# Decay rows picked by matmuls with a single one, and the rounding of whole heads on VectorE, in a fused attention and two-MoE-layer kernel

## The chip, the cores and the metric

One core of one Trainium2 chip. The time is the device time of one execution in microseconds; the runs of a kernel are given by their median. [...]

## The reference

Attention with decay over 4 batches, 8 heads, 576 positions, head size 64, then two feed-forward layers over the 2304 rows of 512 values. All in fp32.

```python
scores = (q @ k.T) / 8
cum    = cumsum(log(clip(f, 1e-4, 1)))            # one row per batch and head
scores = where(causal, -1e9, scores + cum[i] - cum[j])
attn   = softmax(scores);  x = attn @ v           # heads side by side: 2304 x 512
x = (relu(x @ w_in1) ** 2) @ w_out1               # d_ff 2048
x = elu(x @ w_in2) @ w_out2
```

## The kernel before, in words

**Scores with the decay inside.** A head's operand has the 64 rows of q (or k), transposed, and four more rows, 64 to 67, that carry cum and ones, so that one matmul over 68 rows gives scores plus decay. The table `ca` (32 rows, one for each batch and head, with 4 x 512 values: two of 8 cum for q's first 256 columns, two of -8 cum for k's, high and low part of each, ones elsewhere) is made at the start by `split_c` on VectorE (L229 to L232). Positions 256 to 575 have their rows in a DRAM tensor `aug`.

**Two kinds of heads.** Batch 0 is "plain" (`PLAIN = (0,)`): its q and k go into the matmul as fp32, unrounded. Batches 1 to 3 are split: `load_head` with part "F" (a whole head) rounds the raw tile 128x1280 to fp32r into `qk1` (`copy(ENG["qk"][w], ...)`, L126), GpSimd subtracts to get the low parts of q and k (`minus`, L135), a transfer on SP's queue copies k's high part into `qk2`, and another one brings the decay rows. `ENG` says for each step which engine does it for the parts A, B, F: 'a' ScalarE, 'v' VectorE, 'p' GpSimd, 'd' a transfer; `w = "ABF".index(part)`.

**Order of the work.** Batch 0 is done in two passes (`SPLIT = (0,)`): first part A (the first 256 rows) of all eight heads, steps 0 to 7, then for each pair of heads the last 64 rows ("4") and part B. The other batches go through A, A, 4, B, B for each pair. In each step `soft` computes scores, minima and exponentials of one item, `outs` transposes, multiplies by v and folds the item of the step before (`LAG = 1`). Heads are fetched `FETCH = 4` and loaded `AHEAD = 2` steps ahead. Between them `fill()` runs pieces of the first feed-forward layer (`unit`: 256 rows against half of the weights) as a credit by `PACE` and `COST` allows; unit 0 needs all heads of part A. Until it has started, `fill()` issues two or three matmuls on zeros (`busy`, L250), and before everything there are `WARM = 60` of them. From the instructions traced this way a scheduler with a timing model makes each engine's order; an engine runs its instructions in that order.

**Weights.** A half of the first layer's weights comes in as 64-bit words; `words` makes 32-bit ones from it in a tile `wt` (pool `xa`, tag "o", two buffers, shared by other short-lived tiles of that pool): an absolute value on ScalarE (L153), four steps on VectorE (L154 to L157), then rounding on ScalarE (L173) and a subtraction on GpSimd (L135). `W_AT` sets how many halves each step starts.

**The rows of part A.** In `fetch_plain`, for the first head of each pair, SP's queue fetches q and k of both heads (L275) and v (L278) into one tile, and ScalarE's queue issues two transfers (L277) that bring each head's four decay rows from `ca` into partitions 64 to 67 of that tile. `ca` lies one head to a partition, and the four rows must come to four partitions. The scores of part A (`soft_a`, L346) read them.

**Copies.** `copy(eng, dst, x)` is one instruction: ScalarE activation Copy (L126), GpSimd (L128), VectorE tensor_copy (L130). `ps_t` is the PSUM pool with three buffers of tag "t" in which transposes are written.

The lines around the change:

```python
ENG = {'qk': 'aaa', 'ql': 'ppp', 'kh': 'pvd', 'kl': 'ppp', 'vh': 'ppp', 'vl': 'ppp', 'xl': 'pv'}
nc.sync.dma_start(out=t[0:64, 0:1024], in_=first[h // 2])                                         # L275
for i in range(2):
    nc.scalar.dma_start(out=t[64:68, 512 * i:512 * i + 512], in_=f32(ca[g + i:g + i + 1]))       # L277
copy(ENG["qk"][w], qk1, raw[:, ac])                                                              # load_head, part F
```

Of the kernel before, what the change touches and what calls it, by code (L numbers as in the profile page):

```python
# [10 lines left out]
F32 = mybir.dt.float32  # L11
F32R = mybir.dt.float32r
I32 = mybir.dt.int32
AF = mybir.ActivationFunctionType
ALU = mybir.AluOpType

B, H, S, D = 4, 8, 576, 64
# [25 lines left out]
PLAIN = (0,)  # L43

PLAIN_B = 4
CP = {'pA': 'a', 'pB': 'av', 'xA': 'a', 'xB': 'a'}
ENG = {'qk': 'aaa', 'ql': 'ppp', 'kh': 'pvd', 'kl': 'ppp', 'vh': 'ppp', 'vl': 'ppp', 'xl': 'pv'}
NORM = 'ap'
GL = 'pv'
SQ = 'appp'  # L50
# [22 lines left out]
def f32(ap):  # L73
    return ap.bitcast(F32)
# [10 lines left out]
def attention_then_moe_kernel(ctx, tc, first, firstv, plain, qkv, aug0, f, w1, w2, out):  # L85
    nc = tc.nc
    PS = bass.MemoryType.PSUM

    def pool(stack, name, bufs, side, **kw):
        return stack.enter_context(tc.tile_pool(name=name, bufs=bufs, side=side, reuse_waits="tile", **kw))  # L90
# [5 lines left out]
    xa = pool(ctx, "xa", 2, "left")  # L96
# [21 lines left out]
    def minus(eng, dst, x, hi):  # L118
        if eng == "p":
            less(dst, x, hi)  # L120
        else:
            nc.vector.tensor_tensor(dst, x, f32(hi), op=ALU.subtract)

    def copy(eng, dst, x, scale=None):
        if eng == "a":
            nc.scalar.activation(out=dst, in_=x, func=AF.Copy, scale=1.0 if scale is None else scale)  # L126
        elif eng == "p":
            nc.gpsimd.tensor_scalar(dst, x, 1.0 if scale is None else scale, 0.0, op0=ALU.mult, op1=ALU.add)  # L128
        elif scale is None:
            nc.vector.tensor_copy(dst, x)  # L130
        else:
            nc.vector.tensor_scalar(dst, x, scale, None, op0=ALU.mult)
# [65 lines left out]
    ps_t = pool(at, "ps_t", PSB[1], "right", space=PS)  # L198
# [14 lines left out]
    e4s = [a1.tile([128, 640], F32, name=f"e4_{s}") for s in range(2)]  # L213
    me = getattr(nc, MEM)
    ca = wa.tile([B * H, 4, 512], F32R, tag="w7", name="ca")
    me.memset(f32(ca), 1.0)
    nc.gpsimd.memset(mz, 0.0)
    mask(mz[:, 384:512], [[-1, 128]])
# [37 lines left out]
    pairs = {}  # L256

    def fetch_head(b, h, part):
        if b in PLAIN and (part == "A" or h // 2 < PLAIN_B):
            fetch_plain(b, h, part)  # L260
            return
        raw = ab.tile([128, ALL], F32, tag="raw", name="raw", bufs=BUFS["raw"])
        raws[b, h, part] = raw
        nc.sync.dma_start(out=raw, in_=qkv[b, h])

    def fetch_plain(b, h, part):
        g = b * H + h
        k = h % 2
        if part == "A":
            if k == 0:  # L270
                if h // 2 < BUFS["raw"]:
                    t = ab.tile([128, ALL], F32, tag="raw", name="rawA", bufs=BUFS["raw"])
                else:
                    t = hd.tile([128, RAW], F32, tag="qk1", name="rawA", bufs=BUFS["qs"])
                nc.sync.dma_start(out=t[0:64, 0:1024], in_=first[h // 2])  # L275
                for i in range(2):
                    nc.scalar.dma_start(out=t[64:68, 512 * i:512 * i + 512], in_=f32(ca[g + i:g + i + 1]))  # L277
                nc.sync.dma_start(out=t[:, 1024:1280], in_=firstv[h // 2])  # L278
                pairs[b, h // 2] = t
            t = pairs[b, h // 2]  # L280
            raws[b, h, part] = Plain(t, 512 * k - Q0, 512 * k + 256, t[:, 1024 + 128 * k:1152 + 128 * k].rearrange("p (j d) -> p j d", d=D))
            return
        if k == 0:
            t = ab.tile([128, ALL], F32, tag="raw", name="rawB", bufs=BUFS["raw"])
        else:
            t = hd.tile([128, RAW], F32, tag="qk1", name="rawC", bufs=BUFS["qs"])
        nc.sync.dma_start(out=t[0:64, 0:RAW], in_=plain[h])
        nc.sync.dma_start(out=t[64:68, 0:RAW], in_=aug[g])
        if k == 0:
            v = t[:, RAW:ALL]  # L290
        else:
            v = hd.tile([128, 5 * D], F32, tag="vv", name="vp", bufs=BUFS["vv"])
        nc.sync.dma_start(out=v, in_=qkv[b, h, :, RAW:ALL])
        raws[b, h, part] = Plain(t, 0, QW, v.rearrange("p (j d) -> p j d", d=D))

    def aug_split():
        cp, cn = (ab.tile([32, 2, S - 256], F32R, tag="eb", name=t, bufs=BUFS["eb"]) for t in ("cp", "cn"))
        split_c(cp, cn, slice(256, S))
        return cp, cn
# [6 lines left out]
    def load_head(b, h, part):  # L306
# [12 lines left out]
        if part == "A":  # L319
            ac = slice(Q0, QW + 256)  # L320
            copy(ENG["qk"][w], qk1[:, ac], raw[:, ac])
        else:
            ac = slice(0, RAW)
            if part == "F":
                copy(ENG["qk"][w], qk1, raw[:, ac])
            else:
                copy(ENG["qk"][w], qk1[:, qc], raw[:, qc])
                copy(ENG["qk"][w], qk1[:, kc], raw[:, kc])
        if part == "A":
            nc.sync.dma_start(out=f32(qk2[64:68, ac]), in_=f32(ca[g:g + 1]))  # L330
        else:
            nc.sync.dma_start(out=f32(qk2[64:68, ac]), in_=aug[g, :, ac])
        minus(ENG["ql"][w], qk2[0:64, qc], raw[0:64, qc], qk1[0:64, qc])
        if ENG["kh"][w] == "d":
            nc.sync.dma_start(out=f32(qk2[0:64, kc]), in_=f32(qk1[0:64, kc]))
# [8 lines left out]
    def scores(dst, hh, q0, j0, n, first, last):  # L344
        if isinstance(hh, Plain):
            seen[0] = nc.tensor.matmul(out=dst, lhsT=hh.t[0:68, hh.q + q0:hh.q + q0 + 128],  # L346
                                       rhs=hh.t[0:68, hh.k + j0:hh.k + j0 + n], start=first, stop=last)
            return
        qk1, qk2 = hh[0:2]
        nc.tensor.matmul(out=dst, lhsT=qk1[:, q0:q0 + 128], rhs=qk1[:, QW + j0:QW + j0 + n], start=first, stop=False)  # L350
        seen[0] = nc.tensor.matmul(out=dst, lhsT=qk2[0:68, q0:q0 + 128], rhs=qk2[0:68, QW + j0:QW + j0 + n], start=False, stop=last)  # L351

    def reduce_min(e, s, m, nm, init=BIG):
        nc.vector.tensor_tensor_reduce(out=e, in0=s, in1=m, scale=-0.125, scalar=init, op0=ALU.add, op1=ALU.min, accum_out=nm)

    def expo(e, nm, z):
        nc.scalar.activation(out=e, in_=e, func=AF.Exp, bias=nm, scale=-1.0, accum_out=z)
# [7 lines left out]
    def sums(kind, b, hp, k):  # L365
        if k == 0:
            zs[kind, b, hp] = ab.tile([128, 2, 2], F32, tag="z" + kind, name="z" + kind, bufs=3)
        return zs[kind, b, hp][:, :, k]

    def soft_a(b, h, hh):  # L370
        e = ab.tile([128, 384], F32, tag="ea", name="ea", bufs=BUFS["ea"])
        nm = ab.tile([128, 2], F32, tag="nm2", name="nm2", bufs=3)
        z = sums("A", b, h // 2, h % 2)
        s = ps_s.tile([128, 512], F32, tag="s", name="s")
        scores(s[:, 0:256], hh, Q0 + 128, 0, 256, True, True)
        scores(s[:, 256:512], hh, Q0, 0, 256, True, True)
        parts = [slice(0, 256), slice(256, 384)]
        for i, c in enumerate(parts):
            n = c.stop - c.start
            reduce_min(e[:, c], s[:, c], mz[:, 512 - n:512], nm[:, i:i + 1])  # L380
            expo(e[:, c], nm[:, i:i + 1], z[:, i:i + 1])
        return e

    def soft_b(b, h, hh):
        e = ab.tile([128, 896], F32, tag="eb", name="eb", bufs=BUFS["eb"])
        nm = ab.tile([128, 2], F32, tag="nm2", name="nm2", bufs=3)
        z = sums("B", b, h // 2, h % 2)
        parts = [slice(0, 512), slice(512, 896)]
        for i, c in enumerate(parts):
            n = c.stop - c.start  # L390
            s = ps_s.tile([128, 512], F32, tag="s", name="s")
            scores(s[:, 0:n], hh, 128 - 128 * i, 0, n, True, True)
            reduce_min(e[:, c], s[:, 0:n], mz[:, 512 - n:512], nm[:, i:i + 1])
            expo(e[:, c], nm[:, i:i + 1], z[:, i:i + 1])
            yield
        return e
# [142 lines left out]

    def soft(b, hp, kind, k):  # L540
        if kind == "A":
            es[b, hp, kind, k] = soft_a(b, 2 * hp + k, heads[b, hp, k])
            yield
        elif kind == "B":
            es[b, hp, kind, k] = yield from soft_b(b, 2 * hp + k, heads[b, hp, k])
        else:
            e4[b, hp] = soft_4(b, hp, [heads[b, hp, i] for i in range(2)])
            yield
# [180 lines left out]
    for i in range(len(todo) + LAG):  # L729
# [16 lines left out]
        if i < len(todo):  # L746
            sg = soft(*todo[i])
            b, hp, kind, k = todo[i]
        else:
            sg = iter(())  # L750
        if i >= LAG:
            o = todo[i - LAG]
            og = outs(*o)
        else:
            o, og = None, iter(())
# [416 lines left out]
```

## Time and profile before

| | us |
|---|---|
| three timed runs | 1035.57, 1040.85, 1042.72 |
| their median | 1040.85 |
| the profiled execution | 1037.57 |
| its span, first to last instruction | 1035.7 |
| TensorE busy | 1020.5 |
| VectorE busy | 683.1 |
| ScalarE busy | 547.4 |
| GpSimd busy | 275.0 |

PE is TensorE, PEld its weight loads, DVE VectorE, ACT ScalarE, POOL GpSimd, SP the engine whose queue issues most transfers; a q behind the name (ACTq) is the engine's queue at work on something that is not computing, such as issuing a transfer. L277 is line 277 of the kernel. Times in a row are microseconds from the start of the span unless marked ns. Of matmuls the starts are measured and the ends modelled, so that a busy TensorE need not be one at its peak.

### The profile page before, as it was taken

The numbers are of one execution on the slowest core, as the hardware profiler recorded it, in microseconds if no ns is written. First come the engines' busy times: TensorE is split into PE (matmuls) and PEld (weight loads), VectorE is DVE, ScalarE is ACT, GpSimd is POOL, SyncE is SP. The second block draws the span as 40 slices with busy tenths as digits, with TensorE's granted clock in tenths as the row PEclk, the third lists the DMA queues.
The fourth block names the chain that finished last, engine by engine and source line by source line (L and its number), as shares of the span: only waits on it lengthen the run. The fifth ranks groups of instructions, "written<-read, shape, count | busy, mean of one in ns | idle before, by whom it ended". The sixth has DMA issues, their size and how long they took to land.

```text
span 1035.7 us, 17605 instructions
## 1 busy us (share of the span) xinstructions
PE 1020.5 (99%) x6391; PEld 903.5 (87%) x6391; DVE 683.1 (66%) x1543; ACT 547.4 (53%) x1218; POOL 275.0 (27%) x296
## 2 busy tenths in 40 slices
PE   8999999999999999999999999999999999999998
PEld 7676798999999998889988888988988998899897
DVE  4995467665675638847385868896555989754554
ACT  3875688777786734524253535463344565433331
POOL 3565587675776210004103040300000000000000
PEclk8999999999999999999999999999999999999999
DMA  8853645554551164433454555544314465443502
GB/s 247 227 156 109 203 140 170 191 171 145 153 164 54 45 222 137 141 123 143 135 171 170 196 204 199 216 139 179 123 61 158 149 223 170 136 169 124 156 21 82
DMA packets 73881, 158.46 MB, mean 153 GB/s; under 512 B 9316, under 2 KB 34660, under 8 KB 73764
## 3 DMA queue, kind: packets, MB, share of 16 engines
q1 hardware_dynamic: 73732, 157.29, 46.4%
q8 instruction: 50, 0.82, 0.3%
q14 instruction: 35, 0.29, 0.1%
q10 hardware_dynamic: 64, 0.07, 0.0%
HBM read 115.15 MB, written 39.22 MB: 149 GB/s over the span
## 4 chain that ended last, share of the span: by engine, by line
PE 81%; DVE 9%; DMA 3%; POOL 2%; ACT 2%; issue 2%; POOLq 0%; ACTq 0%; DVEq 0%; SPq 0%
PE O L186 29%; PE P L186 16%; PE pH L186 11%; PE o L186 6%; PE ph L186 5%; PE pt L418 4%; PE pv L425 3%; PE s L350 2%; DVE wt L156 2%; PE s L351 2%; PE s L346 1%; DMA x<-yl 1%; PE pv L422 1%; DVE wt L157 1%; POOL qk L135 1%
## 5 line engine op out<-in xcount | busy, mean ns | idle before, releaser
L186 PEld LDWEIGHTS P<-xu,v 128*128 128x128 f32 x1536 | 200.5, 189 | 10.7 <-ACT hs L1013 0.6
L186 PE MATMUL P<-xu,v 128*128 128x256 f32 x1536 | 203.7, 282 | 0.5 <-ACT hs L1013 0.5
L186 PE MATMUL O<-v,gh 128*128 128x512 f32 x576 | 169.2, 393 | 1.4 <-ACT gh L984 1.4
L186 PE MATMUL pH<-xu,w 128*128 128x512 f32 (+1 forms) x672 | 140.8, 360 | 0.0
L186 PEld LDWEIGHTS pH<-xu,w 128*128 128x128 f32 x672 | 114.0, 188 | 20.2
L186 PE MATMUL O<-gh,w 128*128 128x512 f32 (+1 forms) x448 | 122.6, 362 | 0.0
L186 PEld LDWEIGHTS O<-v,gh 128*128 128x128 f32 x576 | 102.8, 188 | 19.4 <-ACT gh L984 1.8
L186 PE MATMUL O<-v,gl 128*128 128x512 f32 x288 | 101.0, 393 | 0.0
L186 PEld LDWEIGHTS O<-gh,w 128*128 128x128 f32 x448 | 79.8, 189 | 14.1
L135 POOL TENSOR_TENSOR yl<-pr,yh 128x512 fp32r<-128x512 f32 x18 | 25.2, 1398 | 249.9 <-ACT yh L833 172.1
L1013 ACT ACTIVATE hs<-P 128x256 f32<-128x256 f32 x128 | 48.0, 381 | 79.5 <-PE P L186 78.8
L135 POOL TENSOR_TENSOR qk<-raw,qk 64x704 fp32r<-64x704 f32 (+1 forms) x48 | 75.7, 1578 | 21.0 <-ACT qk L126 15.7
L186 PE MATMUL O<-gl,w 128*128 128x512 f32 (+1 forms) x224 | 80.1, 363 | 0.0
L1016 DVE TENSOR_TENSOR hs<-P,hs 128x256 f32<-128x256 f32 x96 | 40.4, 422 | 57.9 <-PE P L186 56.0
L186 PE MATMUL o<-gh,w 128*128 128x256 f32 x384 | 75.3, 290 | 0.0
L1038 ACT ACTIVATE g<-g 128x512 f32<-128x512 f32 x64 | 40.2, 629 | 54.8 <-DVE g L1030 32.9
L186 PE MATMUL ph<-xu,w 128*128 128x256 f32 x480 | 67.5, 287 | 1.0 <-DMA xu<-x 0.8
L153 ACT ACTIVATE wt<-wraw 128x512 f32<-128x512 f32 x57 | 38.2, 671 | 55.8 <-DMA wraw<-in_w_dram 42.0
L587 ACT ACTIVATE gh<-g 128x512 fp32r<-128x512 f32 (+1 forms) x80 | 46.9, 586 | 39.3 <-DVE g L586 34.8
L984 ACT ACTIVATE gh<-g 128x512 fp32r<-128x512 f32 x72 | 45.4, 631 | 35.4 <-DVE g L1039 28.6
L586 DVE TENSOR_TENSOR g<-g 128x512 f32<-128x512 f32 (+1 forms) x56 | 45.4, 811 | 26.9 <-ACT g L582 26.7
L186 PEld LDWEIGHTS ph<-xu,w 128*128 128x128 f32 x480 | 60.8, 190 | 1.6 <-DMA xu<-x 1.1
(153 smaller groups left out, 2089.1 us busy)
## 6 DMA issues: line engine op xcount, KB each, us to landing
xu<-x SPq DMA_DIRECT2D x66, 512.0 KB
wraw<-in_w_dram SPq DMA_DIRECT2D x57, 512.0 KB
raw<-in_qkv_dram SPq DMA_DIRECT2D x24, 800.0 KB
x<-yh SPq DMA_DIRECT2D x31, 256.0 KB
x<-yl SPq DMA_DIRECT2D x31, 256.0 KB
x<-xs SPq DMA_DIRECT2D x16, 320.0 KB
xu<-x SPq DMA_DIRECT2D x16, 256.0 KB
raws_w<-in_w_dram SPq DMA_DIRECT2D x7, 512.0 KB
```

Source lines behind the costliest of these rows:

```text
L135: nc.gpsimd.tensor_tensor(out=dst, in0=x, in1=f32(hi), op=ALU.subtract)
L153: nc.scalar.activation(out=f32(t), in_=f32(hi), func=AF.Abs)
L156: nc.vector.scalar_tensor_tensor(t, hi, -0x40000000, t, op0=ALU.bitwise_and, op1=ALU.bitwise_or)
L186: nc.tensor.matmul(out=dst, lhsT=l, rhs=r, start=first and i == 0, stop=last and i == n - 1, skip_group_check=skip)
L418: seen[0] = nc.tensor.transpose(dst, src, ident[:, c0:c0 + 128])
L425: seen[0] = nc.tensor.matmul(out=dst, lhsT=hh[2][:, J, :], rhs=hl[i], start=first and i == 0, stop=last and i == 1)
L586: (nc.vector if sq == "v" else nc.gpsimd).tensor_tensor(out=g[:, 0:n], in0=g[:, 0:n], in1=g[:, 0:n], op=ALU.mult)
L587: nc.scalar.activation(out=gh[:, 0:n], in_=g[:, 0:n], func=AF.Copy)
L984: nc.scalar.activation(out=gh, in_=g, func=AF.Copy)
L1013: nc.scalar.activation(out=o, in_=x, func=AF.Copy)
L1016: nc.vector.tensor_tensor(o, y, x, op=ALU.add)
L1038: nc.scalar.activation(out=gs[i], in_=gs[i], func=AF.Exp)
```

## The change

Three edits. The transfers of `ca` into the tiles of part A (L277) go. In their place `pick_rows(h)` picks head h's four rows by matmuls: a constant `one` (32 x 160, one 1 in each row, at column 67 + 4 x row) is the stationary operand, a window of 128 columns that starts at 4h + 3 - r puts row h of `ca[:, r, :]` into row 64 + r of a PSUM tile, the four products are added up, and rows 64 to 67 are copied into the head's tile, on VectorE for even heads and on ScalarE for odd ones. Heads 0 and 1 are picked before the scores of head 0, and head h + 1 before those of head h. `one` is a tile of the pool `xa` with tag "o", filled by GpSimd. And `ENG["qk"]` changes from 'aaa' to 'aav': the rounding of whole heads (batches 1 to 3) goes from ScalarE to VectorE.

```diff
-ENG = {'qk': 'aaa', 'ql': 'ppp', 'kh': 'pvd', 'kl': 'ppp', 'vh': 'ppp', 'vl': 'ppp', 'xl': 'pv'}
+ENG = {'qk': 'aav', 'ql': 'ppp', 'kh': 'pvd', 'kl': 'ppp', 'vh': 'ppp', 'vl': 'ppp', 'xl': 'pv'}
...
     ca = wa.tile([B * H, 4, 512], F32R, tag="w7", name="ca")
+    one = xa.tile([B * H, 160], F32R, tag="o", name="one")
+    nc.gpsimd.memset(f32(one), 0.0)
+    nc.gpsimd.affine_select(out=one, in_=f32(one), pattern=[[1, 160]], compare_op=ALU.not_equal, fill=1.0, base=-67, channel_multiplier=-4)
     me.memset(f32(ca), 1.0)
...
                 nc.sync.dma_start(out=t[0:64, 0:1024], in_=first[h // 2])
-                for i in range(2):
-                    nc.scalar.dma_start(out=t[64:68, 512 * i:512 * i + 512], in_=f32(ca[g + i:g + i + 1]))
                 nc.sync.dma_start(out=t[:, 1024:1280], in_=firstv[h // 2])
...
+    def pick_rows(h):
+        t, k = pairs[0, h // 2], h % 2
+        pk = ps_t.tile([128, 512], F32, tag="t", name="pk")
+        for r in range(4):
+            c = 4 * h + 3 - r
+            nc.tensor.matmul(out=pk, lhsT=one[:, c:c + 128], rhs=ca[:, r, :], start=r == 0, stop=r == 3)
+        copy("va"[k], t[64:68, 512 * k:512 * k + 512], pk[64:68, :])
...
     def soft(b, hp, kind, k):
         if kind == "A":
+            if b in PLAIN:
+                h = 2 * hp + k
+                for i in ([0, 1] if h == 0 else [h + 1] if h < H - 1 else []):
+                    pick_rows(i)
             es[b, hp, kind, k] = soft_a(b, 2 * hp + k, heads[b, hp, k])
```

## Rows read from the trace of the kernel before

**Rows 1.** The page, busy time of each engine (share of the span) and instructions.
```profile
PE 1020.5 (99%) x6391; PEld 903.5 (87%) x6391; DVE 683.1 (66%) x1543; ACT 547.4 (53%) x1218; POOL 275.0 (27%) x296
```
**Rows 2.** Table by stretches: length, busy time (instructions) of PE, PEld, DVE, ACT, POOL, clock, DMA.
```profile
104.00:130.00 26.00, 26.00 (x160) 19.34 (x159) 11.07 (x40) 16.34 (x42) 13.45 (x16) 1.00 0.61 201
130.00:208.00 78.00, 74.99 (x573) 70.45 (x572) 55.24 (x185) 65.26 (x170) 57.24 (x66) 1.00 0.54 167
208.00:364.00 156.00, 155.80 (x1265) 153.89 (x1264) 97.18 (x296) 117.87 (x292) 93.67 (x105) 1.00 0.38 121
364.00:1035.70 671.70, 665.93 (x3864) 586.12 (x3862) 445.72 (x847) 282.97 (x567) 54.62 (x38) 1.00 0.45 152
```
**Rows 3.** Chain of the whole span, one dense piece: start, length, what.
```profile
431.17 2.81 PE O L186 x12
```
**Rows 4.** Timeline to 49 us: start, length, instruction, [idle before <- what ended it].
```profile
1.05 9.81 PE L250 MATMUL idle<-zero 128*128 128x256 f32 x60 [1.05 <-DVE zero L245]
...
6.98 0.41 DVE L232 SCALAR_TENSOR_TENSOR ca<-cum,ca 32x256 fp32r<-32x256 f32 x1
...
7.46 6.94 ACTq L277 DMA_DIRECT2D rawA<-ca  x6
...
12.56 1.37 PE L346 MATMUL s<-rawA 68*128 68x256 f32 x4 [1.71 <-DMA rawA<-ca]
...
14.09 0.42 DVE L354 CUSTOM_DVE_ANT_0 ea<-s,mz 128x256 f32<-128x256 f32 x1 [5.90 <-PE s L346]
...
14.45 0.66 ACT L153 ACTIVATE wt<-raws_w 128x512 f32<-128x512 f32 x1 [8.77 <-DMA rawA<-ca]
...
48.75 1.33 PE L186 MATMUL ph<-x,w 128*128 128x256 f32 x9
```
**Rows 5.** The table by stretches again, of the first 49 us.
```profile
0.00:10.00 10.00, 8.95 (x55) 8.95 (x56) 4.89 (x11) 3.45 (x4) 5.90 (x23) 1.00 0.80 191
13.00:24.00 11.00, 11.00 (x38) 8.51 (x37) 5.08 (x17) 4.96 (x14) 2.20 (x3) 0.53 0.91 270
24.00:49.00 25.00, 23.71 (x135) 17.11 (x134) 23.52 (x64) 20.77 (x56) 15.18 (x16) 1.00 0.83 232
```
**Rows 6.** Groups by line: line, engine, operation, shapes, count | busy us, mean ns | idle before.
```profile
L126 ACT ACTIVATE qk<-raw 128x1280 fp32r<-128x1280 f32 x24 | 30.5, 1272 | 9.7 <-DMA raw<-in_qkv_dram 6.3 <-PE s L350 1.7 <-PE s L346 1.6
...
L1069 DVE COPY yo<-O 128x512 f32<-128x512 f32 x9 | 6.2, 685 | 1.6 <-DMA part<-yo 1.4
...
L229 DVE TENSOR_SCALAR ca<-cum 32x256 fp32r<-32x256 f32 x1 | 0.3, 305 | 0.1
```
**Rows 7.** Timeline, two waits of TensorE.
```profile
38.56 0.44 PE L418 MATMUL pr<-ident,rb 128*128 128x128 f32 x2 [1.00 <-POOL rb L128]
...
82.32 0.65 PE L422 MATMUL pv<-pp,rawB 128*64 128x192 f32 x4 [2.14 <-DVE pp L130]
```
**Rows 8.** Timeline from 30 to 50 us, weight halves on ScalarE, GpSimd and VectorE.
```profile
32.09 0.68 ACT L153 ACTIVATE wt<-wraw 128x512 f32<-128x512 f32 x1 [0.18 <-POOL w L135]
...
34.07 1.27 POOL L135 TENSOR_TENSOR w<-wt,w 128x512 fp32r<-128x512 f32 x1 [2.01 <-ACT w L173]
34.14 1.49 DVE L155 TENSOR_SCALAR wt<-wt 128x512 int32<-128x512 int32 x1
...
38.47 1.45 POOL L135 TENSOR_TENSOR w<-wt,w 128x512 fp32r<-128x512 f32 x1
```
**Rows 9.** All instructions of line 155: shortest/median/longest in ns, first and last start.
```profile
L155 DVE TENSOR_SCALAR wt<-wt x64: 413/424/1487, 17.3 to 876.0; 128x512 int32<-128x512 int32 x64
```
**Rows 10.** Chain of 156 to 208 us, the rounding of heads in it: start, length.
```profile
160.19 1.17 ACT qk L126
...
195.63 1.16 ACT qk L126
...
199.66 1.16 ACT qk L126
```
**Rows 11.** Waits of ScalarE: who waited for whom, us in total, times, longest.
```profile
ACT qk L126 <- DMA raw<-in_qkv_dram: 6.3, 2, 4.5
```

## Prediction

> **What bounds the kernel now.** I read the busy line of the page first: TensorE is busy for 1020.5 of 1035.7 us [rows 1]. That share alone says little, because a matmul that waits behind another is booked as busy; so I went on to the table by stretches. From 364 us on TensorE is busy for 665.9 of 671.7 us [rows 2], and the chain of the whole span shows what a dense stretch costs: twelve 128x512 matmuls take 2.81 us, 0.234 us each [rows 3]. Nothing the diff edits runs after 364 us, so the change is worth what it takes from, or adds to, the time before that.
>
> Before that there are three stages. Up to 48.75 us, where the first feed-forward matmul starts, batch 0's eight heads of part A run. TensorE warms up on matmuls of zeros until 10.86, is idle for 1.71 us until the decay rows of the first head land, and starts on the scores at 12.56 [rows 4]. [...] From 24 to 49 us VectorE is full, 23.52 of 25.00 us [rows 5]. From 104 to 208 us TensorE still has waits; ScalarE is busy 81.6 of 104.0 us there and VectorE 66.3. From 208 to 364 us TensorE is busy 155.8 of 156.0 us [rows 2]: relief for another engine buys nothing there, only harm would show.
>
> **The change, part by part.**
>
> *The transfers that go.* ScalarE's queue issues row transfers from 7.46 to 14.40 us, and its first own work after them, the first weight half, starts only at 14.45 [rows 4]. Each moves 8 KB (4 x 512 words), so bandwidth gains nothing. The decay table is ready at 6.98 + 0.41 = 7.39 [rows 4], so what replaces the wait has 5 us of room.
>
> *What replaces it on TensorE.* Per head four matmuls of 512 columns, 4 x 0.234 = 0.94 us at full clock [rows 3] (32 rows of contraction instead of 128, taken as no cheaper). They stand behind the warm-up, which ends at 10.86. Heads 0 and 1 are picked before the first scores: 10.86 + 2 x 0.94 = 12.73 us against 12.56 now, +0.2 us. The copy of head 0's rows (0.69 us on VectorE, by the 128x512 copy from PSUM in [rows 6]) runs beside head 1's picks. So the wait is not shortened, it is filled. Were the picks ordered ahead of the warm-up, the scores could start at 7.39 + 0.94 + 0.69 and 0.3 for hand-overs = 9.3 us, 3.2 us earlier; that is an end of the range. The other six heads add 6 x 0.94 = 5.6 us to TensorE's queue before 48.75.
>
> *The clock.* The wait for the rows is TensorE's only idle time between the warm-up and the fall of the clock [rows 4, 5]. [...] TensorE is booked busy all 11 us of the slow stretch at 0.53, so 11 x 0.47 = 5.2 us come back. If the clock falls anyway, three more picks at half clock cost another 3 x 0.94 = 2.8.
>
> *Sum of the first stage.* +0.2 - 5.2 + 5.6 = +0.6. Some picks stand where TensorE waits already; the clearest such wait is 1.0 us at 38.56, for GpSimd [rows 7]. I hide that much: **-0.4 us**. Ends: all 5.6 hidden, -5.0; the clock low and nothing hidden, 0.2 + 5.6 + 2.8 = +8.6.
>
> *Copies and constants.* Eight copies of the rows, at most 0.69 us each, four on VectorE and four on ScalarE. They lie in time that the freed queue gives back: ScalarE had been idle for 8.77 us before 14.45 and VectorE for 5.90 before 14.09 [rows 4]. I cost them at 0; uncovered they would be 8 x 0.69 = 5.5 us. GpSimd's two new instructions on a 32x160 tile join 23 others that take 5.90 of its first 10 us, 0.26 each [rows 5]; with 0.5 more it is still done before 7.39: 0, and 0.5 if it were late.
>
> *Weight halves.* With ScalarE free, the first half can start when it has landed, at about 9 to 10 us (an estimate: by their shapes 1.7 MB are queued up to and with it, and 191 GB/s run in the first 10 us, [rows 5]), some 4 us earlier, and VectorE's four steps on it fill its gap. Against it: the new constant takes one of the two buffers of tag "o" until head 7's picks, and the halves run through these two. The half that starts at 32.09 had waited for GpSimd's subtraction of an earlier one, and its own subtraction runs from 38.47 to 39.92 [rows 8]: 8 us through two buffers, one half every 4 us. Alone in one buffer a half needs some 5.5 us (an estimate: 0.7 to start it, 2.2 on VectorE, 0.6, 1.3, and hand-overs), so by 37 us about five are done, as many as now. What is gained is that VectorE is less full later; the one long wait of TensorE in the following stage is 2.14 us for VectorE at 82.32 [rows 7]. I take half of it: **-1.0 us**. Ends: -2.1; and +4.0, a half late by one spacing.
>
> *The rounding moved to VectorE.* 24 copies of 128x1280, 1272 ns each on ScalarE. VectorE's nearest rows from SBUF: 32x256 in 305 ns [rows 6], 128x512 in 424 [rows 9]: 0.46 ns per column, so 424 + 768 x 0.46 = 780 ns alone. The ends: 0.42 us, and 2.5 times the 685 ns of the copy from PSUM, 1.71. But such an instruction can be held up by GpSimd: the one at 34.14 began 70 ns after a GpSimd subtraction and took 1.49 us, until just after that had ended [rows 8]; the fastest of its kind takes 0.41 [rows 9]. GpSimd is busy 52% to 73% of the time from 104 to 364 us [rows 2]. [...] At worst a copy takes 0.78 + 1.07 = 1.85 us, 24 of them 44 us; VectorE would then be busy 163.5 + 44 = 208 of the 260 us from 104 to 364 [rows 2], still not full, and ScalarE sheds 24 x 1.27 = 30.5. Where it matters: the chain of 156 to 208 us holds the copy three times, 1.16 or 1.17 us each [rows 10], two of them 4 us apart. These two go: **-2.3 us**. Ends: -3.5 with the third, and rival 3. Queueing: VectorE now waits for the raw head's transfer (ScalarE did for 6.3 us in two places, [rows 11]), and behind it stand the softmax's minima and the subtractions of the splits, for which TensorE waits. In ScalarE's queue the exponentials stood in the same place, so I add nothing; at worst 6.3 us. The two GpSimd subtractions and the transfer of each head follow the copy as before.
>
> **Sum.** The profiled execution took 1037.57 us, 1.87 more than its span of 1035.7. -0.4 - 1.0 - 2.3 = -3.7, so 1033.9 in such an execution. The median of the three timed runs, 1040.85, is 3.3 us above it, and gives 1037.2. I say **1036**, between the two; its own range is 1032 to 1040. A measurement of this kernel tells about 1%, 10.4 us, from no change.
>
> **Rivals.**
> 1. *More hides than I allow.* All picks of the first stage (-5.0), all 2.1 us of the wait at 82, and 3.5 in the chain: -10.6, 1027 to 1030. For it: from 24 to 49 us the full engine is VectorE, not TensorE. Against: 32 picks and the fillers of zeros stand in one ordered queue. Chance 0.17.
> 2. *The clock falls all the same,* as it stood at 0.53 for 11 us though TensorE was booked busy throughout [rows 5]. First stage +8.6, the rest -3.3: +5.3, 1043 to 1046. [...] Chance 0.12.
> 3. *VectorE, held by GpSimd, starves TensorE (slower).* One mechanism, from 104 to 364 us: each of the 24 copies waits 1.07 us in VectorE's ordered queue and holds up a minimum or a split that the next matmul needs, 25.7 us in all. Where half of that reaches TensorE, 12.8 us; with -1.4 from the other parts +11.4, 1049 to 1052. It decides from 3.7 us on, some four waits of 24. For it: [rows 8], and a TensorE without slack after 208. Against: VectorE stays under 80%, and heads are prepared two steps ahead. [...] Chance 0.13.
> 4. *It doesn't do what it says:* the filled wait and the freed ScalarE only trade places, 1038 to 1041. Chance 0.13.
>
> My case has 0.45. Faster by over 1% is the better part of rival 1 and a little of my case: 0.14. Slower by over 1% is most of rival 3: 0.09. The rest, 0.77, is within 1%. The range, 1027 to 1047, leaves out rival 3 and the edges of the others.
>
> **What would show it.** No transfers in ScalarE's queue at 7.46; picks from 10.9; first scores near 12.7; granted clock 1.00 from 13 to 24; first feed-forward matmul near 48; first weight half near 10; VectorE's copies of qk near 0.8 us, some up to 1.9; VectorE's busy time up by 20 to 35 us, ScalarE's down by some 28; TensorE still without a gap from 208 to 364. I am wrong if the clock stays at 0.53 up to 24 us, if the first feed-forward matmul moves by more than 4 us, or if copies hold up minima and TensorE shows idle time after 208.

## The result, and the profile after

The changed kernel takes 1051.5 us (median of 15 runs, 1043.0 to 1058.25) against 1041.64 before (15 runs, 1035.57 to 1044.1): a ratio of 1.0105, 95% interval 1.0084 to 1.0126. It is about 10 us slower, and outside the range I gave. A granted clock of 1.00 is TensorE's full one, 0.50 half of it: the trace of the kernel before has 1.00 from 10 to 13 us and 0.50 from 14 to 23. The runs of one kernel differ by TensorE's mean granted clock: after the change from 1043.0 us at 0.998 to 1058.25 at 0.984. At 0.998 the kernel before takes 1036.2 to 1038.2 us (twelve executions) and the changed one 1043.0 and 1045.2 (two), so some 6 to 8 us of the loss stand at an equal clock and the rest comes with a lower one.

The profiled execution took 1047.1 us (span 1045.2), and its clock is a high one for this kernel, 0.996. The busy line answers [rows 1]: VectorE +26, as forecast, and ScalarE -21, where I had some 28.

```profile
PE 1028.1 (98%) x6423; PEld 908.2 (87%) x6423; DVE 709.0 (68%) x1571; ACT 526.0 (50%) x1198; POOL 280.8 (27%) x298
```

Its timeline of the first stage answers [rows 4]:

```profile
10.42 0.66 ACT L153 ACTIVATE wt<-raws_w 128x512 f32<-128x512 f32 x1 [5.03 <-DMA raws_w<-in_w_dram]
...
10.70 3.05 PE L305 MATMUL pk<-ca,one 32*128 32x512 f32 x12
11.11 0.43 DVE L154 TENSOR_SCALAR wt<-wt 128x512 f32<-128x512 f32 x1 [3.06 <-ACT wt L153]
11.57 0.43 DVE L155 TENSOR_SCALAR wt<-wt 128x512 int32<-128x512 int32 x1
...
12.03 0.69 DVE L156 SCALAR_TENSOR_TENSOR wt<-raws_w,wt 128x512 int32<-128x512 int32 x1
12.76 0.69 DVE L157 SCALAR_TENSOR_TENSOR wt<-raws_w,wt 128x512 int32<-128x512 int32 x1
...
13.48 1.29 DVE L130 COPY rawA<-pk 4x512 f32<-4x512 f32 x2
...
14.22 1.13 PE L358 MATMUL s<-rawA 68*128 68x256 f32 x4 [0.47 <-DVE rawA L130]
...
50.93 1.29 PE L186 MATMUL ph<-x,w 128*128 128x256 f32 x7
```

Two things differ from what I laid out. Twelve picks stand ahead of the first scores, not eight: the scheduler put head 2's there too. And the copy of head 0's rows, whose picks are the first four of the twelve and done about 1 us after 10.70, stands in VectorE's queue behind all four steps on the first weight half; ScalarE takes that half up at 10.42 only because its queue is free now. So the scores start at 14.22, not 12.73, and TensorE waits 0.47 us for VectorE.

The table by stretches answers [rows 5] and [rows 2] (columns as there):

```profile
13.00:24.00 11.00, 10.53 (x57) 7.84 (x55) 7.08 (x23) 7.73 (x21) 3.44 (x4) 1.00 1.04 313
24.00:49.00 25.00, 24.92 (x130) 17.49 (x129) 19.71 (x54) 18.26 (x50) 10.51 (x13) 1.00 0.68 187
49.00:104.00 55.00, 51.34 (x291) 36.75 (x289) 43.77 (x87) 33.68 (x75) 33.34 (x30) 0.97 0.45 136
...
208.00:364.00 156.00, 155.80 (x1261) 153.76 (x1261) 107.78 (x319) 108.12 (x287) 99.53 (x112) 1.00 0.39 125
```

In this execution the clock did stay at 1.00 through the first stage (0 to 49 us), and the first feed-forward matmul still comes 2.2 us later than before (50.93 against 48.75). From 24 to 49 us TensorE is now the full engine, 24.92 of 25.00, and VectorE has 5.3 us of air; before, both were nearly full, VectorE with 23.52 and TensorE with 23.71 us [rows 5]. From 208 to 364 nothing changed, 155.80 us busy in both.

The next loss is where before there was one wait [rows 7]. TensorE's waits from 78 to 104 us:

```profile
83.86 0.65 PE L434 MATMUL pv<-pp,rawB 128*64 128x192 f32 x4 [1.09 <-DVE pp L130]
...
90.50 0.75 PE L434 MATMUL pv<-pp,vp 128*64 128x320 f32 x2 [2.18 <-ACT xB L126]
```

And the chain of that stretch (start, length, what):

```profile
80.37 1.67 DVE wt L156
...
82.06 1.41 DVE wt L157
83.47 0.33 DVE pp L130
...
84.58 1.23 DVE wt L155
...
85.83 1.65 DVE wt L156
...
88.09 0.60 DVE wt L157
...
89.37 0.76 ACT e L126
90.13 0.33 ACT xB L126
...
90.50 0.75 PE pv L434 x2
```

The chain runs through the weight halves on VectorE: they are late. The last half is done at 90.8 us against 87.5 before. Behind the second wait the clock falls for a short time (0.50 from 92 to 94 us, 0.97 over the row from 49 to 104). TensorE's matmuls fall from 2.3 us behind (first matmul of the second layer, 86.89 against 84.63) to 5.3 (first scores of batch 1, 122.11 against 116.85), and stay there to 357.08 against 351.87. First scores of batch 1, before and after:

```profile
116.85 0.28 PE L350 MATMUL s<-qk 128*128 128x256 f32 x1
```
```profile
122.11 0.28 PE L362 MATMUL s<-qk 128*128 128x256 f32 x1
```

What comes after that, up to the 9.5 us between the two spans, is the least certain part: experiment 10 shows two such places without any of the change.

### The profile page after: what moved, and what is told of

Same layout as the page of the kernel before. It is cut to its first block, busy times and chain, and to the rows that moved or that the text cites. A ratio compares the mean times of both kernels' runs of the same rounds, so it can differ in the third digit from the quotient of the medians.

```text
span 1045.2 us, 17679 instructions
## 1 busy us (share of the span) xinstructions
PE 1028.1 (98%) x6423; PEld 908.2 (87%) x6423; DVE 709.0 (68%) x1571; ACT 526.0 (50%) x1198; POOL 280.8 (27%) x298
## 4 chain that ended last, share of the span: by engine, by line
PE 88%; DVE 5%; DMA 3%; issue 1%; POOL 1%; ACT 1%; SPq 1%; DVEq 0%; POOLq 0%; ACTq 0%
PE O L186 31%; PE P L186 17%; PE pH L186 13%; PE o L186 6%; PE ph L186 5%; PE pt L430 4%; PE pv L437 4%; PE s L362 2%; PE s L363 2%; PE pv L434 2%; PE s L358 1%; DVE wt L156 1%; DMA x<-yl 1%; DVE wt L157 1%; POOL qk L135 1%
## 5 line engine op out<-in xcount | busy, mean ns | idle before, releaser
L186 PEld LDWEIGHTS P<-xu,v 128*128 128x128 f32 x1536 | 201.2, 189 | 11.6 <-DVE hs L1032 0.7
L186 PEld LDWEIGHTS o<-gh,w 128*128 128x128 f32 x384 | 60.7, 191 | 3.1 <-issue 3.0
```

Of the source, the lines that this page charges most:

```text
L186: nc.tensor.matmul(out=dst, lhsT=l, rhs=r, start=first and i == 0, stop=last and i == n - 1, skip_group_check=skip)
```

## The experiments

Theories: V, VectorE held by GpSimd (my rival 3); N, the picks' own time on TensorE; C, the clock falls when TensorE waits for the copied rows; L, the first scores come late because the copies stand behind the weight steps; and B, the buffer of tag "o" that the new constant takes from the weight halves. The first expectations call N by the letter Q. Ratios are against the kernel before, run on the same chip (medians 1040.7 to 1041.3).

**1. The rounding alone** (before, with `ENG["qk"] = 'aav'`).

> Only the rounding of whole heads goes to VectorE; decay rows come by transfers as before. Theory B (the shared buffer of tag o delays the weight halves): same as before within 3 us, weight halves as before, last one done near 87 us. Theory V (VectorE held by GpSimd starves TensorE): 5 to 10 us slower than before, with new waits of TensorE after 104 us. Theory Q (picks fill TensorE's queue): same as before.

1041.65 us, ratio 1.0002 (0.9983 to 1.0022). In its groups by line:

```profile
L130 DVE CAST qk<-raw 128x1280 fp32r<-128x1280 f32 x24 | 23.7, 987 | 8.0 <-DMA raw<-in_qkv_dram 7.6 <-PE s L350 0.3
```

VectorE takes the copies at no cost and no gain. V falls as a cause of the loss, and so does my gain of 2.3 us.

**2 to 4. The picks alone (2); the change with a tile of its own for the constant (3); both (4).** The edit of 3 and 4 gives the constant a buffer of another tag, which the feed-forward layer first writes at 70.6 us in experiment 3:

```diff
-    one = xa.tile([B * H, 160], F32R, tag="o", name="one")
+    one = mg.tile([B * H, 160], F32R, tag="gl", name="one")
```

> Only the picks; rounding stays on ScalarE; the constant keeps its place in tag o. Theory B: 7 to 11 us slower than before, like the whole change, last weight half done near 90 us, TensorE idle between 80 and 95 us and the granted clock at 0.50 once more there. Theory V: same as before within 3 us. Theory Q: 2 to 4 us slower than before.

> The whole change, with the constant in a buffer of the feed-forward's tag gl, so that both buffers of tag o serve the weight halves. Theory B: 8 to 12 us faster than the whole change, at before or up to 3 us faster, weight halves done by 83 to 86 us and no fall of the clock between 80 and 95 us. Theory V: still 8 to 10 us slower than before. Theory Q: 2 to 4 us slower than before.

> Picks with the constant in tag gl and rounding on ScalarE. Theory B: as e3_own_tile within 3 us. Theory V: same as before, and 8 us faster than e3_own_tile. Theory Q: 2 to 4 us slower than before.

| | tag "o" | own tile |
|---|---|---|
| rounding on ScalarE | 1051.18, 1.0093 (1.0063 to 1.0123) | 1046.08, 1.0056 (1.0035 to 1.0077) |
| rounding on VectorE | 1051.5, 1.0105 (the change) | 1046.39, 1.0062 (1.0044 to 1.008) |

Rows alike, columns 5 us apart (some 4 by the ratios): the picks cost some 5.5 us, the shared buffer 4 to 5 more. Neither B alone, which expected 8 to 12 us back from experiment 3, nor N alone, with a loss of 2 to 4, had this. The traces show the second directly: the pair of waits at 83.86 and 90.50 (1.09 and 2.18 us) stands in the picks alone too, at 98.02 and 104.64 with 1.07 and 2.16; with the tile of its own one wait is left:

```profile
82.30 0.75 PE L434 MATMUL pv<-pp,rawB 128*64 128x320 f32 x2 [0.27 <-DVE pp L130]
```

Its last weight half is done at 83.9 us, not 90.8. The table by stretches of the picks alone (experiment 2) shows what the picks meet at the lower clock:

```profile
13.00:24.00 11.00, 9.62 (x29) 7.23 (x29) 5.51 (x16) 4.82 (x13) 2.16 (x3) 0.59 1.04 316
24.00:45.00 21.00, 21.00 (x64) 14.62 (x63) 7.43 (x23) 9.04 (x26) 3.83 (x5) 0.50 0.35 97
```

TensorE is booked busy for all 21 us at a granted clock of 0.50, while VectorE, nearly full before (19.52 us of the same stretch), is busy for a third of the time. A TensorE without a gap in the record is thus not by itself at the higher clock, so the time at either clock is read from rows.

**5, 6. The wait filled; no fillers.** Both on experiment 3, in `pick_rows` for 5 (`last` is the pick before), in the constants for 6.

```diff
+        if h == 1:
+            with tc.issue_after(last.ins):
+                busy(16)
```
```diff
-WARM, FILL, FILL_TO = 60, 2, 14
+WARM, FILL, FILL_TO = 60, 2, 0
```

> e3_own_tile with 16 more matmuls of zeros (1.9 us at full clock) behind the picks of heads 0 and 1, where TensorE otherwise waits for the copies of the rows. They only add work. Theory C (the wait for the copies lets the clock fall, and at half clock picks and fillers make TensorE the bound): 4 to 8 us faster than e3_own_tile, 1038 to 1042, granted clock 1.00 from 15 to 30 us. Theory N (too many matmuls in the queue, whatever the clock): 0 to 2 us slower than e3_own_tile. Theory L (the later first scores cost, nothing else): same as e3_own_tile.

> e3_own_tile without the 59 matmuls of zeros between the steps of part A; the 60 at the start stay. Theory N: 5 to 8 us faster than e3_own_tile. Theory C: the clock falls at least as often and stays down longer, 0 to 6 us slower than e3_own_tile unless the shorter queue makes up for it. Theory L: same as e3_own_tile.

Filled: 1046.89, 1.0056 (1.003 to 1.0082), the clock over the span mostly higher (median 0.995 against 0.992) and the time the same, where C expected 4 to 8 us less. Its trace shows that the wait was moved more than filled: TensorE runs without a gap from 10 to 18 us and the clock stays up (1.00 from 10 to 20 us), but then it waits for 1.74 us, the clock falls behind this wait, and the first feed-forward matmul comes at 60.00 us, 57.04 in experiment 3. From its chain, and its table by stretches:

```profile
18.46 1.74 issue
```
```profile
15.00:20.00 5.00, 3.46 (x18) 2.64 (x16) 4.87 (x8) 1.42 (x4) 2.12 (x2) 1.00 1.11 286
20.00:25.00 5.00, 4.81 (x20) 3.63 (x21) 4.16 (x13) 4.92 (x14) 2.26 (x3) 0.78 0.97 292
25.00:30.00 5.00, 5.00 (x17) 3.38 (x17) 2.08 (x7) 2.64 (x8) 1.67 (x2) 0.54 0.90 260
```

What ends that wait the profile does not name. Without the fillers of zeros (four executions): 1051.43, 1.0106 (1.0065 to 1.0148), clock 0.978 to 0.98. Its row of the table by stretches, from 24 to 49 us:

```profile
24.00:49.00 25.00, 25.00 (x63) 14.89 (x62) 15.69 (x40) 14.22 (x38) 8.70 (x9) 0.50 0.67 190
```

So the fillers are not the load that could be dropped; without them the clock stays low longer (0.50 over the row from 24 to 49 us, 0.89 in experiment 3).

**7, 8. Four heads picked at once; the same with a shorter warm-up.** Both on experiment 3. Ones 32 columns apart put four heads' rows at partitions 0, 32, 64 and 96: 8 picks instead of 32.

```diff
-    nc.gpsimd.affine_select(out=one, in_=f32(one), pattern=[[1, 160]], compare_op=ALU.not_equal, fill=1.0, base=-67, channel_multiplier=-4)
+    nc.gpsimd.affine_select(out=one, in_=f32(one), pattern=[[1, 260]], compare_op=ALU.not_equal, fill=1.0, base=-3, channel_multiplier=-32)
...
-            c = 4 * h + 3 - r
+            c = 128 * g + 3 - r
...
-        copy("va"[k], t[64:68, 512 * k:512 * k + 512], pk[64:68, :])
+        for q in range(4):
+            t, k = pairs[0, 2 * g + q // 2], q % 2
+            copy("va"[k], t[64:68, 512 * k:512 * k + 512], pk[32 * q:32 * q + 4, :])
```

Experiment 8 has this and `WARM = 36`.

> e3_own_tile with picks for four heads at once: the constant has its ones 32 columns apart, so that the rows of four heads come to partitions 0, 32, 64 and 96 of one PSUM tile; 8 matmuls of 512 columns in place of 32, the same eight copies. Theory N: 4 to 7 us faster than e3_own_tile (24 x 0.234 us at full clock, twice that at half). Theory C: as far as the clock still falls, the picks no longer double the stage: 3 to 6 us faster than e3_own_tile, still at or above before. Theory L: 1 us faster.

> e7_four_heads with 36 warm-up matmuls in place of 60, so that the picks start when the table is ready, near 8 us. Theory L: 2 to 3 us faster than e7_four_heads. Theory C: the wait of TensorE before the first scores stays or grows, and the clock falls in it as often or more: 0 to 3 us slower than e7_four_heads. Theory N: 1 to 2 us faster than e7_four_heads.

7: 1045.73, 1.0046 (1.0029 to 1.0063), hardly better than 32 picks, where N expected 4 to 7 us: TensorE waits 3.48 us for the copy, which stands behind the weight steps. So N alone does not hold. 8: 1040.51, 0.9991 (0.9969 to 1.0013). With picks from 6.87 us the copies stand ahead of the weight steps, and the scores start at 9.08, not 14.45. That looked like L; experiment 11 tests it with all 32 picks.

**9. All copies on ScalarE** (the whole change, 60 warm-up matmuls).

```diff
-        copy("va"[k], t[64:68, 512 * k:512 * k + 512], pk[64:68, :])
+        copy("a", t[64:68, 512 * k:512 * k + 512], pk[64:68, :])
```

> The whole change, but all eight copies of the decay rows on ScalarE, so that the copy of head 0 no longer stands behind VectorE's four steps on the first weight half. Theory L (the late first scores, 14.2 to 14.8 us, cost time, in place and through the clock): first scores at 12.4 to 12.9 us, 1.5 us earlier than in the changed kernel, the wait of TensorE before them under 1 us; the time falls by 1 to 4 us against the changed kernel (1051.5) to 1047 to 1050, still above the kernel before for the buffer of tag o. Theory N (the picks' own TensorE time is the cost, wherever the first scores stand): no change, 1050 to 1053.

1045.85, 1.0058 (1.0028 to 1.0088): 5.7 us better than the change, more than expected. Its timeline:

```profile
11.61 0.59 ACT L126 ACTIVATE rawA<-pk 4x512 f32<-4x512 f32 x1 [0.40 <-PE pk L305]
...
13.36 1.13 PE L358 MATMUL s<-rawA 68*128 68x256 f32 x4
```

The copy is done before the twelve picks are, and TensorE goes on without a wait, so 13.36 is the picks' doing (10.37 + 2.99), not the copy's. Six of ten runs have a clock of 0.994 or more, of the change's 15 three. Two late waits are still there (0.58 at 80.74, for ScalarE, and 1.73 at 90.32): the buffer is still shared.

**10. The kernel before with a longer warm-up.**

```diff
-WARM, FILL, FILL_TO = 60, 2, 14
+WARM, FILL, FILL_TO = 76, 2, 14
```

> The kernel before with 76 warm-up matmuls in place of 60, so that its wait of 1.71 us for the decay rows is filled with work and nothing else of the change is in it. Warm-up ends near 13.5 us, first scores then at 13.5 instead of 12.56. My forecast's clock step (the wait makes the clock fall, 5.2 us come back when it is filled): granted clock 1.00 from 13 to 24 us and the time 3 to 5 us below the kernel before. Rival (the clock falls because of what TensorE does after the warm-up, whatever stands in the wait): clock at 0.5 for about as long as before, time 0 to 2 us above the kernel before.

1038.72, 0.9979 (0.9958 to 1.0): 2.1 us faster, where I expected 3 to 5, and at the edge of its interval; all ten runs at a clock of 0.996 to 1.0. Its row of the table by stretches, from 13 to 24 us:

```profile
13.00:24.00 11.00, 10.83 (x62) 8.89 (x63) 8.10 (x29) 8.94 (x27) 4.51 (x5) 1.00 0.87 253
```

And its timeline, first scores and first feed-forward matmul:

```profile
13.10 1.10 PE L346 MATMUL s<-rawA 68*128 68x256 f32 x4 [0.28 <-DMA rawA<-ca]
...
44.52 1.34 PE L186 MATMUL ph<-x,w 128*128 128x256 f32 x9
```

My clock step in the kernel before, by itself: the wait filled but for 0.28 us, the clock at 1.00 from 13 to 24 us, and the first feed-forward matmul 4.2 us earlier (44.52 against 48.75), though the scores start 0.5 later. In the medians half of that shows. By its mean clock, not every execution of the kernel before loses it: at 0.998 that kernel takes 1036.2 to 1038.2 us, and this kernel, with more warm-up, 1038.1 to 1040.0. It is also the measure of the picks at an equal clock: with them the same matmul stands at 50.47 (experiment 9), 6.0 us later. And its timeline shows the losses behind 364 us with no pick in the kernel:

```profile
364.63 0.48 PE L186 MATMUL o<-gh,w 128*128 128x256 f32 x2 [1.22 <-DVE xB L450]
...
675.91 3.50 PE L186 MATMUL O<-v,gh 128*128 128x512 f32 x8 [1.91 <-ACT gh L984]
```

The changed kernel's profile has the same two, 1.22 us at 373.23 and 1.91 at 684.33, and both kernels run at a clock of 0.83 for 10 us around the second. The profile of before has the second wait alone, 1.40 us, and no fall of the clock. So of the 9.5 us between the two profiles some 4 (9.5 - 5.2) are of a kind that comes without the change.

**11, 12. 32 picks started early; 8 picks with the wait filled.** 11 is experiment 3 with 24 warm-up matmuls; 12 is experiment 8 with `W_AT = (0, 1, 1, 1, 1, 0, ...)` for `(1, 1, 1, 1, 0, 0, ...)` and 8 matmuls of zeros after the first picks.

> The whole change with its constant in a tile of its own and 24 warm-up matmuls, so that the picks start as soon as the table is ready and the copies stand ahead of the weight steps on VectorE; all 32 picks stay. Against the run with four heads at a time and a short warm-up (1040.5, eight picks) it differs in the number of picks. First scores at 9 to 10.5 us. Theory L (the late start is the cost): 1040 to 1043, most of the loss gone although all picks are there. Theory N (the picks are the cost): 1045 to 1047, as with 60 warm-up matmuls.

> Picks of four heads at a time, 36 warm-up matmuls, the start of weight halves one step later (none in step 0, one in step 4), and 8 matmuls of zeros between the first picks and the first scores, so that TensorE does not wait for the copies. Theory C (the wait for the copies makes the clock fall): granted clock 1.00 through the first 25 us or low for one stretch of 7 us at most, time 1035 to 1039, below the kernel before. If the clock falls as in the run without these matmuls (13.65 us at 0.50): 1039 to 1042, no difference from the kernel before.

11: 1046.62, 1.0047 (1.0025 to 1.0068): the scores start at 10.30, 4.5 us earlier than in experiment 3, and nothing is gained. L as the whole cause falls. N fits, but this run does not part it from the clock, which fell earlier here than in experiment 3 (1.00 there from 10 to 15 us, 0.50 from 20 to 25, 1.00 again from 30 to 35) and stayed low longer (median over the span 0.987 against 0.992), though no wait of TensorE from 5.9 to 49 us is longer than 0.18 us:

```profile
10.00:24.00 14.00, 14.00 (x40) 10.10 (x40) 7.26 (x20) 7.07 (x17) 3.54 (x4) 0.50 1.05 324
24.00:49.00 25.00, 25.00 (x118) 18.23 (x117) 19.15 (x47) 15.85 (x44) 8.84 (x10) 0.84 0.57 170
```

Against the kernel before, in medians, 32 picks cost 5.7 us (3), fewer picks alone 4.4 (7), an early start alone 5.8 (11), and with both 0.8 are gained (8). Neither gains alone what they gain together.

12: 1037.53, 0.9965 (0.9949 to 0.9981), 3.3 us faster than the kernel before and 14 faster than the change. Every run has a clock of 0.995 or more. The scores start at 9.98. Its table by stretches:

```profile
13.00:24.00 11.00, 10.01 (x40) 7.18 (x39) 9.61 (x26) 7.38 (x20) 3.56 (x4) 0.69 1.05 312
24.00:49.00 25.00, 22.79 (x124) 15.98 (x124) 23.74 (x57) 19.03 (x53) 13.70 (x15) 1.00 0.76 216
```

VectorE is the fuller engine again. Only the wait before the first scores is filled: two later ones stand (0.82 us before 12.19 and 0.99 before 14.66), and the clock still falls, to a mean of 0.69 from 13 to 24 us. The edit of `W_AT` was not run apart, so which of the two edits gained the 2 to 3 us on experiment 8 stays open.

**13, 14. Both mends; the change once more.** 13 is experiment 9 with the constant's own tile.

> The whole change with both mends at once: the constant in a tile of its own and all eight copies of the decay rows on ScalarE; the 32 picks and 60 warm-up matmuls stay. If the loss is a sum of three (the picks' own time on TensorE, the buffer of tag o, the clock lost by the wait for a copy), the buffer's 4 us go against the run with the copies on ScalarE alone (1045.85) and the clock is up as often as there: 1041 to 1043, the first feed-forward matmul near 50.5, TensorE's lag behind the kernel before not growing from 85 to 101 us. Rival (the two mends take away the same microseconds, the late halves being only a consequence of the late start): 1045 to 1047.

> The changed kernel itself once more, for a trace of an execution with the lower clock that most of its runs show (0.984 to 0.992 over the span). If such a run has its clock fall in the first stage: granted clock 0.5 from about 14 us for 20 us or more, TensorE booked busy without a gap in that time, first feed-forward matmul at 57 us or later, 1050 to 1057 us. If the clock falls elsewhere (after 50 us, or late in the program): the first feed-forward matmul near 51 as in the profile of the changed kernel, and the half-clock stretches stand later.

13: 1044.38 over ten executions; 1.003 (1.0009 to 1.005) without one of 1058.15 us, whose clock is 0.98. That lies between the two expectations. No wait of TensorE is left from 78 to 104 us, so the buffer's part is gone for itself. But the clock is not mended, as three narrow stretches of its table show:

```profile
10.90:13.00 2.10, 2.10 (x10) 1.70 (x10) 1.61 (x4) 1.45 (x3) 0.00 (x0) 1.00 1.03 412
13.60:14.10 0.50, 0.50 (x2) 0.00 (x0) 0.50 (x2) 0.20 (x1) 0.00 (x0) 0.50 1.04 418
24.00:30.00 6.00, 6.00 (x22) 4.45 (x21) 1.12 (x5) 3.31 (x9) 2.26 (x2) 0.50 0.72 235
```

Here it fell while TensorE was in its picks, with no gap before. C in its plain form, a wait and then a fall, is not the whole of it, here as in experiment 11.

14: one execution of the change at 0.992, 1051.55 us, close to the median. Its timeline, first scores and first feed-forward matmul:

```profile
14.41 0.92 PE L358 MATMUL s<-rawA 68*128 68x256 f32 x3 [0.96 <-DVE rawA L130]
...
57.32 0.93 PE L186 MATMUL ph<-x,w 128*128 128x256 f32 x4
```

And its table by stretches:

```profile
13.00:24.00 11.00, 10.04 (x34) 7.49 (x34) 5.54 (x16) 5.53 (x15) 2.67 (x4) 0.63 1.04 303
24.00:49.00 25.00, 25.00 (x124) 18.06 (x122) 15.39 (x42) 14.84 (x42) 8.25 (x10) 0.89 0.55 154
```

The wait for the copy is 0.96 us instead of 0.47, the clock falls (0.63 from 13 to 24 us), TensorE has no gap from 24 to 49 us, and the first feed-forward matmul is 8.6 us late. The first scores of batch 1 are 11.6 us late (128.47 against 116.85): the rest is the pair of waits again, 1.09 and 2.17 us at 90.26 and 96.89.

## Why the prediction was wrong

**The clock: the failed step.** My sum takes 5.2 us back from the slow stretch, 13 to 24 us at 0.53 [rows 5]: with the wait filled I expected 1.00 there. In the kernel before this holds (experiment 10: 1.00 from 13 to 24 us, 4.2 us at the first feed-forward matmul; I had 5.2). But the change does not fill the wait. I let the copy of head 0's rows run beside head 1's picks and never asked what stands ahead of it in VectorE's queue, although I had the first weight half arrive at about 10 us two paragraphs on, with VectorE's four steps "to fill its gap". They filled the place of the copy. TensorE waits 0.47 us (the profile after) or 0.96 (experiment 14) before its first scores, and mostly the clock falls: 12 of the 15 executions have a mean clock of 0.992 or less, as experiment 14 has, whose trace shows the fall. What exactly decides it stays open: it fell in experiment 13 without a gap and in experiment 11 with none over 0.18 us, and it stayed up behind the 0.47 us of the profile after and in most runs of experiment 9 (six of ten have a mean clock of 0.994 or more), whose order on TensorE at the start is the same.

**First stage: +8.6, my end of the range.** At the lower clock and with nothing hidden I had 0.2 + 5.6 + 2.8 = 8.6; experiment 14 shows 57.32 - 48.75 = 8.6. That the two agree is in part luck, for the terms differ: head 2's picks, ahead of the scores, belong to the start, which is 1.9 us late in place of 0.2. Where the clock stayed up (the profile after) the terms are a start 1.7 later, 4.8 us of clock (4.2 and the 0.5 of the later start in experiment 10), and five heads of four picks at 0.254 us, 5.1: 1.7 - 4.8 + 5.1 = 2.0, and 2.2 were measured. So the picks' price held, and none of it was hidden: from 24 to 49 us TensorE, not VectorE, is full now. I had let them hide in a wait of the kernel before, and had called VectorE the full engine of that stretch, though the same row has TensorE busy for 23.71 of 25.00 us [rows 5].

**Weight halves: wrong sign.** I took -1.0, with an end of +4.0 for a half late by one spacing. Measured: +3 us. From the first feed-forward matmul to the first scores of batch 1 the kernel before takes 68.1 us, the change 71.2 in both of its traces. With the tile of its own it takes 65.9 (experiment 3, from 57.04 to 122.97, so with the start of experiment 14): the buffer costs 5.2 us by the traces, and 5.1 by the medians of experiments 2 to 4. "About five halves done by 37 us, as many as now" was right in that the count is the same (but four in both) and missed what the one buffer does: the halves go one at a time until head 7's picks are done at 36.2, the fifth half's subtraction starts at 41.27 us against 38.47 before, and most of the later ones stay some 3 us late up to the last, so that VectorE's steps on them stand ahead of the copies TensorE needs.

**Rounding: -2.3 became 0.** The size was right, 0.78 us and up to 1.85 forecast. All 24 copies of the profile after, shortest/median/longest in ns, first and last start:

```profile
L130 DVE CAST qk<-raw x24: 808/834/1830, 93.7 to 322.2; 128x1280 fp32r<-128x1280 f32 x24
```

The longest, 1830 ns against the 1.85 us I had as the worst, starts at 146.49 us, while GpSimd's two subtractions of 144.42 are running, and ends 0.68 us after them (148.32 against 147.64). That costs nothing: the rounding alone is at 1.0002 (experiment 1). What failed is the gain. In the chain of 156 to 208 us after, which answers [rows 10], the copy is there four times (start, length):

```profile
160.88 0.91 DVE qk L130
...
179.48 0.74 DVE qk L130
...
182.94 1.30 DVE qk L130
...
201.03 0.75 DVE qk L130
```

A copy on the chain of a stretch moves with its engine and stays on the chain, 3.70 us in four pieces now for 3.49 in three before; I had counted two of the three as gone.

**Transfers, copies, constants** held: ScalarE's first half starts at 10.42, GpSimd's constant is ready at 4.04, the copies cost 690 ns. That the copies cost nothing was wrong through their place, not their length.

**The rivals.** Rival 2 was the right mechanism for the first stage, at a chance of 0.12, and too cheap by 6 us: it carried my gains of 3.3 us along (weights and rounding), where 3 us of loss stood. With 8.6 + 3.0 it gives 1037.57 + 11.6 = 1049.2; the 2.4 us that experiment 14 loses between the last scores of the split heads (363.42 against 351.87) and the end of the span (1049.7 against 1035.7) are the rest to 1051.5. Where the clock stayed up in the first stage (the profile after), the 9.5 us are 2.2 there, 3.0 for the weight halves, and 4.3 behind 357 us, where I had nothing; of the terms of my sum the weight halves are there the one missed by most, by 4.0 us. Rival 3 had the time, 1049 to 1052, with a mechanism that the runs exclude.

## What to carry to other kernels

When an edit frees one engine, follow what that engine then does earlier into every ordered queue behind it: here weight steps came early and stood ahead of a four-row copy that the first matmuls needed. A "free" buffer of a shared tag is not free if its lifetime spans the stage that streams through it; putting a constant of 640 bytes in each of 32 partitions elsewhere was worth 4 to 5 us. And work added to TensorE should be priced at its lower clock too, where TensorE may become the bound: in the chain of experiment 3 four picks take 2.00 us at 20.82, at a clock of 0.50, and 1.12 at 33.18, at 1.00. Eight picks in place of 32, started early, with the first wait filled, the constant moved and the weight halves begun a step later, turned a loss of 10 us into a gain of 3.3; neither fewer picks nor the early start did this alone.

## What the runs showed of the hardware that I had not expected

A TensorE that is booked busy without a gap can stay at half clock for long: 21.00 of 21.00 us at 0.50 in experiment 2, 25.00 of 25.00 in experiment 6. The lower clock can also set in without a gap (experiment 13, between 13.0 and 13.6 us, in the middle of the picks). And one program, run again, differs by as much as 15 us, and the time goes with the clock: the change took 1043.0 us at a mean clock of 0.998 and 1058.25 at 0.984.
